# Block-recurrent attention with a mixture-of-depths layer: some turns moved from TensorE to VectorE and through DRAM

## The chip, the cores and the metric

One core of a Trainium2 chip runs the whole kernel. The metric is the device time of one execution in microseconds (us).

## The reference

For 8 batches (B) and 8 heads, x holds 512 rows and the state 32 rows of 64 values. All is float32.

```
scores  = x @ state.T / 8;  a  = softmax(scores);   xread = a @ state     # 512 rows a head
scores2 = state @ x.T / 8;  a2 = softmax(scores2);  sread = a2 @ x        # 32 rows a head
x2[b]   = rows of xread and sread, heads side by side                     # 544 x 512
s       = x2[b] @ w_gate;  top = the 128 rows with the highest s
out[b]  = x2[b];  out[b, top] += sigmoid(s[top]) * (relu(x2[b, top] @ w1) @ w2)   # w1 512x1024, w2 1024x512
```

## The kernel before

Each batch goes through two parts.

*Attention.* x of a batch is loaded as `xf`, 128 partitions by heads, 4 row groups and 64 values. TensorE turns it with the identity, four 128x128 blocks at a time (`turn`, L350), and ScalarE takes each group out of PSUM into `xT` (L359). `scores` (L380) writes scores of both directions into PSUM, state rows on the partitions. For the x rows VectorE turns the scores in 32x32 blocks (L398), takes maximum, difference, sum and product (L402 to L417) and turns them back into `eT` (L420); `read` (L464) makes xread. For the state rows VectorE takes the maximum (L426) and ScalarE the exponential `a` (L430). The second product needs `a` with the x rows on the partitions: TensorE turns it in two groups of four blocks (`turn` in `attention`, L488), ScalarE copies each to `aT` (L491), and `state_read` (L504) makes sread, which ScalarE scales into `xt` (L510). SP stores xread rows (`x_rows`, L531, one DMA) and sread rows (`s_rows`, L536, four DMAs) to the output.

*Choice and layers.* VectorE ranks the rows (`win`, L596; one-hot, L634), TensorE picks the row numbers (L650), POOL gathers the 128 chosen rows back from the output into `xr` (L543). TensorE turns them (L719) into `xg`, the first layer (L736) and the second layer (L753) follow, VectorE adds (`ot`, L756), POOL scatters the rows (L543). The layers are run for batches 0, 1 and 2, 3 and 4, 5 and 6, and 7, two batches side by side as 256 columns.

*The order.* Every step is recorded by `add` with an engine, an assumed length, what it comes after, which buffers it takes and uses, and, for a DMA, how long its data lands after issue (`lands`). `carry_out` then writes all queues out: at each turn it takes the engine that can start first, and on it, among the steps that can start by then, the one with the lowest key, batch number plus an offset by name (`LATER`). The layers have offsets of 100, so that they fill what attention leaves free. A step that waits for a step of another engine counts that step's landing, a step on the same engine does not:

```python
        def since(p, q):
            return end[q] + HOP if q.engine != p.engine else done[q]
```

The queues are in order on the chip. While the first PSUM buffer of the layers is not taken, idle times of TensorE in the plan are filled with small turns of the identity (L160).

Of the kernel before, what the change touches and what calls it, by code (L numbers as in the profile page):

```python
# [8 lines left out]
F32 = mybir.dt.float32  # L9
# [9 lines left out]
def kernel(  # L19
# [10 lines left out]
    nc = tc.nc  # L30
# [4 lines left out]
    SP = S + Ns  # L35
# [19 lines left out]
    def pool(name, bufs, **kw):  # L55
        return ctx.enter_context(tc.tile_pool(name=name, bufs=bufs, **kw))

    N_X, N_XR = 5, 8
    DV = D + 1
    COPIED = ()  # L60
    const = pool("const", 1)
    xin = pool("xin", N_X)
    work = pool("work", 1)
    small = pool("small", 6)
    psum = pool("psum", 1, space=bass.MemoryType.PSUM)


    ctx.enter_context(tc.manual_schedule(engines={ENG.PE, ENG.DVE, ENG.Activation, ENG.SP, ENG.Pool}))
# [3 lines left out]
    SOON = {"PE": 0.0000, "DVE": 0.6720, "ACT": 0.0000, "POOL": 0.0000, "SP": 0.3000, "DMA": 0.0000}  # L72

    LATER = {
        "add": -100.0000, "below": 5.0000, "exp": 5.0000, "exps": -1.1961, "fetch": -2.0379, "first": 100.0000,
        "gate": 0.1040, "gate_s": -0.2629, "heads": -0.5574, "in": -1.6252, "index": -4.8083, "inverse": -1.5775,
        "load": -50.0000, "load_x": -2.0000, "max": 5.0000, "mult": -1.1840, "numbers": 2.7643, "off": -5.0000,
        "oh": -0.9823, "out": -2.8554, "over": -4.8131, "parts": -4.8782, "pick": 3.7775, "picked": -2.5156,
        "plus": -1.1285, "put": -100.0000, "read": 2.4337, "relu": -100.0000, "row": -5.0000, "row_kept": 4.5966,
        "row_s": -4.3556, "row_s_kept": 2.7056, "rows": -4.2797, "score_s": 2.6270, "scores": 1.6993,  # L80
        "second": 100.0000, "sexp": -2.1366, "sigmoid": 4.8122, "smax": -0.6190, "sread": -3.1166, "srows": 2.9423,
        "ssum": -2.6238, "state_T": -4.7221, "state_gates": 2.5691, "states": 1.3988, "store": 3.0032,
        "sub": -4.1349, "sum": -0.5374, "tables": 0.2302, "turn": 0.9682, "turn_a": -2.8074, "turned": -3.8777,
        "turned_a": 3.0201, "twice": 2.0508, "win": -4.7738, "xg": 90.0000, "xg_kept": -100.0000,
    }
    class Buf:

# [12 lines left out]
    class Piece:  # L100
        def __init__(self, engine, length, fn, after, takes, uses, key, lands):
            self.engine, self.length, self.fn, self.lands = engine, length, fn, lands
            self.name, self.key = key[1], key[0] + LATER.get(key[1], 0.0)
            self.after, self.takes, self.uses = [p for p in after if p], takes, uses
            for buf in list(takes) + list(uses):
                buf.users.append(self)
# [58 lines left out]
    def sbuf(name, shape, bufs, dtype=F32, where=None):  # L165
        return Ring(name, shape, dtype, bufs, where)
# [2 lines left out]
    P_SO = Ring("ps_so", [128, 2048], F32, 1, psum)  # L169
    P_H = Ring("ps_h", [128, 512], F32, 2, psum)  # L170
    R_X = Ring("xf", [128, H, NC, D], F32, N_X, xin)
    R_XT = sbuf("xT", [128, 2, 2, 128], 12)
    R_SC = sbuf("s_c", [128, 1024], 1)
    R_E = sbuf("e", [128, 32, Ns], 2)
    R_A = sbuf("a", [128, 2, 2, 256], 1)
    R_ET = sbuf("eT", [128, 2, 2, 2, 128], 2)
    R_AT = sbuf("aT", [128, NC, 128], 2)
    R_XS = sbuf("xs", [128, NC, Dm], 2)
    R_ROW = sbuf("srow", [128, SP], 1)
    R_WIN = [sbuf(f"win{c}", [128, SP - first[c]], 1, BF16) for c in range(NC + 1)]  # L180
# [155 lines left out]
    def attention(b):  # L336

        def key(n):
            return (b, n)
# [3 lines left out]
        for pair in range(H // 2):  # L343
            ps, t = Buf(P_TR), Buf(R_XT)

            def turn(pair=pair, ps=ps):
                v = ps.ap.rearrange("p (k r t) -> p k r t", k=2, r=2)
                for k in range(2):
                    for r in range(2):
                        nc.tensor.transpose(v[:, k, r], xf[b].ap[:, 2 * pair + k, 2 * r:2 * r + 2].rearrange("p w d -> p (w d)"), ident)  # L350

            on = "DVE" if b == 0 and pair % 2 else "ACT"

            def keep(ps=ps, t=t, on=on):
                v = ps.ap.rearrange("p (k r t) -> p k r t", k=2, r=2)
                if on == "DVE":
                    nc.vector.tensor_copy(out=t.ap, in_=v)
                else:
                    nc.scalar.copy(out=t.ap, in_=v)  # L359

            px = p_x[b]
            p = add("PE", 0.66 if b else 0.9, turn, after=[px[(pair * len(px)) // (H // 2)]] + last_turn[-1:], takes=[ps, t], uses=[xf[b]],
                    key=key("turn"))
            last_turn.append(p)
            p_xT.append(add(on, 0.6, keep, after=[p], uses=[ps, t], key=key("turned")))
            xT.append(t)
# [14 lines left out]
                                         xT[2 * g + q // 2].ap[half, q % 2].rearrange("p r t -> p (r t)"),  # L381
                                         start=True, stop=True)

        p_s = add("PE", 1.09, scores, after=p_xT + [p_sT[b]], takes=[s], uses=xT, key=key("scores"))
        if b in COPIED:
            p_s = add("ACT", 1.1, lambda: nc.scalar.copy(out=s_c.ap, in_=s_p.ap[:, 0:1024]), after=[p_s], takes=[s_c], uses=[s],
                      key=key("s_kept"))
# [91 lines left out]
                                uses=[o] + ([xs] if c else []), key=key("rows")))  # L479

        aT, p_aT = [], []
        for g in range(2):
            ps, t = Buf(P_TR), Buf(R_AT)

            def turn(g=g, ps=ps):
                v = ps.ap.rearrange("p (c m) -> p c m", c=NC)
                for c in range(NC):
                    nc.tensor.transpose(v[:, c], a.ap[:, g, c % 2, 128 * (c // 2):128 * (c // 2 + 1)], ident)  # L488
# [23 lines left out]
        p = add("PE", 1.1, state_read, after=p_aT, takes=[o2], uses=aT + [xf[b]], key=key("sread"))  # L512
# [189 lines left out]
    def layers(units, number):  # L702
# [7 lines left out]
        n = at[-1]  # L710
        xg, hT = Buf(R_XG), Buf(R_HT)
        p_xg = []
        for u, lo in zip(units, at):
# [7 lines left out]
            def keep(m=m, pt=pt, lo=lo):  # L721
                nc.scalar.copy(out=xg.ap[:, :, lo:lo + m], in_=pt.ap.rearrange("p (j s) -> p j s", j=ND)[:, :, 0:m])
# [97 lines left out]
```

## Time and profile before

| | |
|---|---|
| median of 3 runs | 217.89 us (217.42 to 218.48) |
| the profiled execution | 215.81 us |
| its span, first to last instruction | 214.0 us |
| granted TensorE clock | 0.999 |
| busy: TensorE, VectorE, ScalarE, POOL | 203.1, 116.3, 89.5, 48.2 us |
| moved by DMA | 26.61 MB, mean 124 GB/s |

The page gives the busy time of each engine, then the span in 40 slices of 5.35 us (a digit is the busy share in tenths), the DMA queues, the chain of work that ended last, the costliest groups and the DMA issues. PE is TensorE's matmul, PEld its weight load, DVE VectorE, ACT ScalarE, SP SyncE; SPq is SP's queue of DMA issues. A float32 matmul of the layers shows as two records, a turn as one.

### The profile page before, as it was taken

Reading aid. Unit: us, or ns where it says so; the run is one execution under the profiler, and the core shown is the slowest. Engines: PE = TensorE matmul, PEld = TensorE weight load, DVE = VectorE, ACT = ScalarE, POOL = GpSimd, SP = SyncE. Lnnn points to the kernel's source line nnn. Section 1 sums busy time; section 2 is a strip of 40 time slices with the busy share of each in tenths; the row PEclk is TensorE's granted clock in tenths of the full one; section 3 lists DMA queues with packets and bytes.
Section 4 is the critical chain, followed back from the end, with each engine's and each line's share of the span. In section 5 each row is a group of like instructions: output and inputs, shape, how many; then the busy total and the mean of one; then the engine's idle time right before and its main releaser. Section 6 shows DMA issues by size and latency. Waiting matters only on the chain.

```text
span 214.0 us, 5364 instructions
## 1 busy us (share of the span) xinstructions
PE 203.1 (95%) x2230; PEld 146.2 (68%) x2230; DVE 116.3 (54%) x271; ACT 89.5 (42%) x196; POOL 48.2 (23%) x139
## 2 busy tenths in 40 slices
PE   6989899999999999999999999999999999999990
PEld 5767676789875568978647667887554887447830
DVE  1499989876686974639987665883340100011001
ACT  2388886973556653534637423534410012000200
POOL 8002010510453021060243115233106200022001
PEclk9999999999999999999999999999999999999999
DMA  7999999629521014043021326102402100011001
GB/s 197 319 307 390 391 360 384 204 77 318 212 54 49 15 49 191 8 142 122 0 61 52 133 83 247 49 9 55 199 0 87 61 3 0 0 49 49 0 0 49
DMA packets 17407, 26.61 MB, mean 124 GB/s; under 512 B 5608, under 2 KB 13800, under 8 KB 16360
## 3 DMA queue, kind: packets, MB, share of 16 engines
q1 hardware_dynamic: 15304, 21.70, 29.4%
q0 software_dynamic: 1280, 4.20, 6.1%
q10 hardware_dynamic: 800, 0.39, 0.7%
q8 instruction: 17, 0.28, 0.6%
q14 instruction: 6, 0.05, 0.1%
HBM read 15.27 MB, written 11.01 MB: 123 GB/s over the span
## 4 chain that ended last, share of the span: by engine, by line
PE 55%; issue 22%; POOL 8%; DVE 6%; ACT 6%; DMA 2%; POOLq 1%; ACTq 0%
PE ps_h L736 14%; PE ps_h L753 13%; PE ps_so L464 7%; PE ps_tr L350 4%; PE ps_tr L504 3%; PE ps_so L380 3%; PE ps_tr L488 3%; POOL xr L543 2%; POOL out_dram L543 2%; ACT a L430 2%; DMA xf<-in_state_dram 2%; PE ps_tr L577 2%; PE ps_tr L623 1%; PE ps_tr L719 1%; ACT xT L359 1%
## 5 line engine op out<-in xcount | busy, mean ns | idle before, releaser
L736 PE MATMUL ps_h<-xg,w 128*128 128x256 f32 (+1 forms) x320 | 60.7, 342 | 0.0
L753 PE MATMUL ps_h<-w,hT 128*128 128x512 f32 x128 | 58.8, 600 | 0.0
L736 PEld LDWEIGHTS ps_h<-xg,w 128*128 128x128 f32 x320 | 50.3, 191 | 6.0 <-issue 1.4
L753 PEld LDWEIGHTS ps_h<-w,hT 128*128 128x128 f32 x128 | 23.0, 190 | 22.9 <-issue 22.5
L756 DVE SCALAR_TENSOR_TENSOR ot<-ps_h,z,xr 128x512 f32<-128x512 f32 x8 | 6.0, 751 | 45.6 <-PE ps_h L753 45.6
L740 ACT ACTIVATE hT<-ps_h 128x512 f32<-128x512 f32 x16 | 9.5, 596 | 44.5 <-PE ps_h L736 44.5
L596 DVE SCALAR_TENSOR_TENSOR win<-srow,sc,after 128x544 bf16<-128x544 f32 (+4 forms) x40 | 18.2, 511 | 15.7 <-ACT srow L586 15.7
L543 POOL DMA_INDIRECT out_dram<-ot,idx x8 | 9.6, 1203 | 63.2 <-DVE ot L756 45.8
L468 ACT COPY xs<-ps_so 128x512 f32<-128x512 f32 x32 | 17.5, 589 | 14.4 <-PE ps_so L464 10.3
L350 PE MATMUL ps_tr<-ident,xf 128*128 128x128 f32 x128 | 20.8, 297 | 0.7 <-ACT xT L359 0.4
L359 ACT COPY xT<-ps_tr 128x512 f32<-128x512 f32 x30 | 17.2, 590 | 7.6 <-PE ps_tr L350 7.0
L464 PE MATMUL ps_so<-st_v,eT 32*128 32x65 f32 x512 | 18.0, 276 | 1.2 <-ACT a L430 0.9
L350 PEld LDWEIGHTS ps_tr<-ident,xf 128*128 128x128 f32 x128 | 14.7, 148 | 6.1 <-ACT xT L359 1.5
L464 PEld LDWEIGHTS ps_so<-st_v,eT 32*128 32x128 f32 x512 | 15.8, 186 | 4.4 <-ACT a L430 1.3
L430 ACT ACTIVATE a<-ps_so,nm 128x512 f32<-128x512 f32 x16 | 10.9, 688 | 7.4 <-DVE nm L426 6.6
L543 POOL DMA_INDIRECT xr<-out_dram,idx x8 | 9.9, 1231 | 16.0 <-DVE sc L566 8.3
L398 DVE STREAM_TRANSPOSE e<-ps_so 128x1024 f32<-128x1024 f32 x8 | 9.9, 1240 | 2.1 <-PE ps_so L380 1.9
L412 DVE TENSOR_REDUCE sm<-e 128x32 f32<-128x1024 f32 x8 | 9.6, 1205 | 2.5 <-ACT e L408 2.5
L420 DVE STREAM_TRANSPOSE eT<-e 128x1024 f32<-128x1024 f32 x8 | 9.9, 1243 | 0.2
L417 DVE TENSOR_TENSOR e<-e,sm 128x1024 f32<-128x1024 f32 x8 | 9.8, 1225 | 0.3
L405 DVE TENSOR_TENSOR e<-e,mx 128x1024 f32<-128x1024 f32 x8 | 9.8, 1223 | 0.2
L488 PE MATMUL ps_tr<-ident,a 128*128 128x128 f32 x64 | 9.5, 280 | 0.3 <-ACT a L430 0.2
(86 smaller groups left out, 220.5 us busy)
## 6 DMA issues: line engine op xcount, KB each, us to landing
out_dram<-xs SPq DMA_DIRECT2D x8, 1024.0 KB, 4.5
xf<-in_x_dram SPq DMA_DIRECT2D x14, 512.0 KB, 7.5
w<-in_moe_w_dram SPq DMA_DIRECT2D x2, 2048.0 KB, 15.7
xf<-in_x_dram SPq DMA_DIRECT2D x3, 256.0 KB, 4.0
out_dram<-xt SPq DMA_DIRECT2D x32, 16.0 KB, 2.8
xf<-in_state_dram SPq DMA_DIRECT2D x1, 384.0 KB, 8.7
xf<-in_x_dram ACTq DMA_DIRECT2D x1, 256.0 KB, 4.6
xf<-in_state_dram ACTq DMA_DIRECT2D x1, 128.0 KB, 3.6
```

What stands on the lines that cost most here:

```text
L350: nc.tensor.transpose(v[:, k, r], xf[b].ap[:, 2 * pair + k, 2 * r:2 * r + 2].rearrange("p w d -> p (w d)"), ident)
L359: nc.scalar.copy(out=t.ap, in_=v)
L398: nc.vector.transpose(out=flat(e), in_=s.ap[:, 0:1024])
L420: nc.vector.transpose(out=eT.ap.rearrange("p w g r t -> p (w g r t)"), in_=flat(e))
L430: nc.scalar.activation(out=a.ap[:, g], in_=view_s()[:, :, g], func=AF.Exp, bias=tmp["nm"][:, g:g + 1], accum_out=tmp["ss"][:, g:g + 1])
L464: nc.tensor.matmul(view(o)[:, q, c - c0, g], eT.ap[r, c % 2, g, c // 2], st_v[r, b, g], start=True, stop=True)
L468: nc.scalar.copy(out=xs.ap[:, c].rearrange("p (g q m) -> p g q m", g=2, q=4), in_=view(o)[:, :, c - c0, :, 0:D].rearrange("p q g m -> p g ...
L488: nc.tensor.transpose(v[:, c], a.ap[:, g, c % 2, 128 * (c // 2):128 * (c // 2 + 1)], ident)
L543: touches(b, nc.gpsimd.indirect_dma_start(**kw), True)
L596: nc.vector.scalar_tensor_tensor(wins[c].ap[0:n], srow.ap[0:n, f:SP], sc[0:n, b, c:c + 1], after[0:n, 0:SP - f], op0=ALU.is_gt, op1=ALU.mu ...
L736: nc.tensor.matmul(v[:, f, 0:n], w1[:, j, 128 * (f0 + f):128 * (f0 + f + 1)], xg.ap[:, j, 0:n], start=(j == 0), stop=(j == ND - 1))
L753: nc.tensor.matmul(py.ap[0:m], hT.ap[:, f, lo:lo + m], w2[:, f], start=(f == 0), stop=(f == NF - 1))
```

## The change

x of batches 6 and 7 is loaded a second time (`load_x2`), in four DMAs a batch of 2048 pieces of 128 bytes, so laid out that VectorE's turn of 32x32 blocks gives `xT` at once. TensorE's turns and ScalarE's copies of these batches are gone; `xf` is still loaded.

`a` of batches 3 to 7 is turned by VectorE in 32x32 blocks into `a_b` (two instructions). The blocks then stand on the wrong partitions: SP stores `a_b` (512 KB) to a DRAM buffer `a_d` and loads it back in four DMAs of 1024 pieces of 128 bytes, each to 32 partitions of `aT2`, which `state_read` uses.

`xg` is laid out with the two batches apart, so that the first layer's moving operand is two runs of 128 columns in place of one of 256. A path that would turn `xr` the same way (`XG_BLOCKS`) is there and empty. Rings of `xT` and `xr` become shorter. Steps of batches 3 and up get names with `_b` and offsets of their own in `LATER`, so the planner writes another order.

```diff
-    N_X, N_XR = 5, 8
+    N_X, N_XR = 5, 6
     DV = D + 1
+    ON_DVE = (6, 7) if cap <= 128 else ()
+    A_BLOCKS = (3, 4, 5, 6, 7) if cap <= 128 else ()
+    XG_BLOCKS = () if cap == 128 else ()
...
+        "a_in_b": 1.5525, "a_out_b": -0.7448, "add": -100.0000, "add_b": -100.0000, "below": 5.0000,
...
-            self.name, self.key = key[1], key[0] + LATER.get(key[1], 0.0)
+            self.name = key[1] + ("_b" if key[0] >= 3 else "")
+            self.key = key[0] + LATER.get(self.name, LATER.get(key[1], 0.0))
...
-    R_XT = sbuf("xT", [128, 2, 2, 128], 12)
+    R_XT = sbuf("xT", [128, 2, 2, 128], 9)
+    R_X2 = sbuf("x2", [128, 2, H, 4, 32], 1)
+    R_AB = sbuf("a_b", [128, 2, NC, 4, 32], 1)
+    R_AT2 = sbuf("aT2", [128, 2, NC, 128], 1)
+    R_AD = Ring("a_d", [128, 2 * NC * 128], F32, 2, dram)
-    R_XG = sbuf("xg", [128, ND, 256], 1)
+    R_XG = sbuf("xg", [128, 2, ND, 128], 1)
...
+    def load_x2(b, key):
+        buf = x2[b] = Buf(R_X2)
+        p_x2[b] = []
+        for w in range(2):
+            for e in range(2):
+                def go(w=w, e=e):
+                    src = x[b].rearrange("h (s t r w) (e d) -> w e t r h s d", s=4, t=32, r=2, e=2)[w, e]
+                    o = 32 * (2 * w + e)
+                    nc.sync.dma_start(out=buf.ap[o:o + 32], in_=src)
+                p_x2[b].append(add("SP", 1.8, go, after=[p_scores[b - 2]], takes=[] if p_x2[b] else [buf],
+                                   uses=[buf] if p_x2[b] else [], key=key, lands=5.0))
...
+            if b in ON_DVE:
+                def turn_blocks(pair=pair, t=t):
+                    nc.vector.transpose(out=t.ap.rearrange("p k r t -> p r k t"),
+                                        in_=x2[b].ap[:, :, 2 * pair:2 * pair + 2].rearrange("p r k s d -> p r k (s d)"))
+                p_xT.append(add("DVE", 0.64, turn_blocks, after=p_x2[b], takes=[t], uses=[x2[b]], key=key("blocks")))
+                xT.append(t)
+                continue
...
+        if b in A_BLOCKS:
+            a_b, a_d, aT2 = Buf(R_AB), Buf(R_AD), Buf(R_AT2)
+            def turn_blocks_a(g):
+                nc.vector.transpose(out=a_b.ap[:, g].rearrange("p (r w) k n -> p w r (k n)", w=2),
+                                    in_=a.ap[:, g].rearrange("p w (r t) -> p w r t", r=2))
+            def a_out():
+                nc.sync.dma_start(out=a_d.ap, in_=a_b.ap.rearrange("p g c k n -> p (g c k n)"))
+            def a_in():
+                for k in range(4):
+                    src = a_d.ap.rearrange("(q t) (z k n) -> k t z q n", q=4, k=4, n=32)[k]
+                    nc.sync.dma_start(out=aT2.ap[32 * k:32 * (k + 1)].rearrange("p g c (q n) -> p (g c) q n", q=4), in_=src)
+            for g in range(2):
+                p_aT.append(add("DVE", 0.66, lambda g=g: turn_blocks_a(g), after=[p_a[g]], takes=[] if g else [a_b],
+                                uses=[a] + ([a_b] if g else []), key=key("blocks_a")))
+            p = add("SP", 0.6, a_out, after=p_aT, takes=[a_d], uses=[a_b], key=key("a_out"), lands=2.2)
+            p_aT = [add("SP", 2.8, a_in, after=[p], takes=[aT2], uses=[a_d], key=key("a_in"), lands=3.0)]
-        for g in range(2):
+        for g in range(0 if b in A_BLOCKS else 2):
...
+                w = lambda j: w1[:, j, 128 * (f0 + f):128 * (f0 + f + 1)]
+                if n == 256:
+                    parts = [(v[:, f].rearrange("p (k s) -> p k s", k=2), xg.ap)]
+                else:
+                    parts = [(v[:, f, at[k]:at[k + 1]], xg.ap[:, k:k + 1, :, 0:u["m"]]) for k, u in enumerate(units)]
...
+        if b in ON_DVE:
+            load_x2(b, (b, "load_x2"))
```

More of the change, by code (lines that the diff above doesn't have):

```diff
@@ L65 @@
     psum = pool("psum", 1, space=bass.MemoryType.PSUM)
+    dram = pool("dram", 1, space=bass.MemoryType.DRAM)
     ctx.enter_context(tc.manual_schedule(engines={ENG.PE, ENG.DVE, ENG.Activation, ENG.SP, ENG.Pool}))
@@ L74 @@
     LATER = {
[L75 to L84, printed above, removed]
+        "a_in_b": 1.5525, "a_out_b": -0.7448, "add": -100.0000, "add_b": -100.0000, "below": 5.0000,
@@ new lines @@
+        "below_b": 4.9516, "blocks_a_b": -3.1491, "blocks_b": 4.2830, "exp": 5.0000, "exp_b": 1.6188,
+        "exps": -1.1961, "exps_b": 1.5285, "fetch": -2.0379, "fetch_b": -4.0717, "first": 100.0000,
+        "first_b": 100.0000, "gate": 0.1040, "gate_b": -0.1483, "gate_s": -0.2629, "gate_s_b": 3.5004,
+        "heads": -0.5574, "heads_b": -4.7153, "in": -1.6252, "in_b": -3.5996, "index": -4.8083, "index_b": -3.6051,
+        "inverse": -1.5775, "inverse_b": 2.5077, "load": -50.0000, "load_x2_b": 1.9782, "load_x_b": -2.2786,
@@ new lines @@
+        "max": 5.0000, "max_b": 4.6396, "mult": -1.1840, "mult_b": 3.4491, "numbers": 2.7643, "off": -5.0000,
+        "off_b": 4.2618, "oh": -0.9823, "oh_b": 4.0841, "out": -2.8554, "out_b": -4.5034, "over": -4.8131,
+        "over_b": 2.4833, "parts": -4.8782, "parts_b": 0.9309, "pick": 3.7775, "pick_b": 4.5229, "picked": -2.5156,
+        "picked_b": 4.7396, "plus": -1.1285, "plus_b": -1.3919, "put": -100.0000, "put_b": -100.0000,
+        "read": 2.4337, "read_b": 4.8884, "relu": -100.0000, "relu_b": -100.0000, "row": -5.0000, "row_b": 2.4330,
@@ new lines @@
+        "row_kept": 4.5966, "row_kept_b": 3.0545, "row_s": -4.3556, "row_s_b": -2.7187, "row_s_kept": 2.7056,
+        "row_s_kept_b": 1.4228, "rows": -4.2797, "rows_b": 4.7760, "score_s": 2.6270, "score_s_b": -4.6623,
+        "scores": 1.6993, "scores_b": 4.0082, "second": 100.0000, "second_b": 100.0000, "sexp": -2.1366,
+        "sexp_b": 1.8469, "sigmoid": 4.8122, "sigmoid_b": 0.5311, "smax": -0.6190, "smax_b": 3.6740,
+        "sread": -3.1166, "sread_b": 3.0414, "srows": 2.9423, "srows_b": 0.4806, "ssum": -2.6238, "ssum_b": -0.7188,
@@ new lines @@
+        "state_T": -4.7221, "state_T_b": -3.3351, "state_gates": 2.5691, "state_gates_b": 4.7733, "states": 1.3988,
+        "states_b": 4.5170, "store": 3.0032, "store_b": 1.3222, "sub": -4.1349, "sub_b": -4.5526, "sum": -0.5374,
+        "sum_b": -2.8598, "tables": 0.2302, "turn": 0.9682, "turn_a": -2.8074, "turn_b": 3.1911, "turned": -3.8777,
+        "turned_a": 3.0201, "turned_b": 3.5876, "twice": 2.0508, "win": -4.7738, "win_b": -5.0000, "xg": 90.0000,
+        "xg_b": 90.0000, "xg_kept": -100.0000, "xg_kept_b": -100.0000,
@@ L177 @@
     R_AT = sbuf("aT", [128, NC, 128], 2)
+    R_AB = sbuf("a_b", [128, 2, NC, 4, 32], 1)
+    R_AT2 = sbuf("aT2", [128, 2, NC, 128], 1)
+    R_XB = sbuf("x_b", [128, ND, 4, 32], 1)
+    R_AD = Ring("a_d", [128, 2 * NC * 128], F32, 2, dram)
+    R_XD = Ring("x_d", [128, Dm], F32, 2, dram)
     R_XS = sbuf("xs", [128, NC, Dm], 2)
@@ L266 @@
     make_identity(nc, ident)
-    xf, p_x, last_load = {}, {}, []
+    xf, p_x, last_load, x2, p_x2, p_scores = {}, {}, [], {}, {}, {}
     def load_x(b, key, pieces=2):
@@ L382, in scores @@
                                          start=True, stop=True)
-        p_s = add("PE", 1.09, scores, after=p_xT + [p_sT[b]], takes=[s], uses=xT, key=key("scores"))
+        p_s = p_scores[b] = add("PE", 1.09, scores, after=p_xT + [p_sT[b]], takes=[s], uses=xT, key=key("scores"))
         if b in COPIED:
@@ L503, in state_read @@
                         rr = slice(Ns * q, Ns * (q + 1))
-                        nc.tensor.matmul(o2.ap[rr, D * g:D * (g + 1)], aT[g].ap[:, c, rr], xf[b].ap[:, 4 * g + q, c],
+                        nc.tensor.matmul(o2.ap[rr, D * g:D * (g + 1)], (aT[g].ap if aT else aT2.ap[:, g])[:, c, rr], xf[b].ap[:, 4 * g + q, c],
                                          start=(c == 0), stop=(c == NC - 1))
@@ L510, in state_rows @@
                 nc.scalar.activation(out=tmp["xt"][:, g], in_=o2.ap[:, D * g:D * (g + 1)], func=AF.Copy, scale=tmp["rs"][:, g:g + 1])
-        p = add("PE", 1.1, state_read, after=p_aT, takes=[o2], uses=aT + [xf[b]], key=key("sread"))
+        p = add("PE", 1.1, state_read, after=p_aT, takes=[o2], uses=(aT or [aT2]) + [xf[b]], key=key("sread"))
         p_xt = add("ACT", 0.42, state_rows, after=[p, p_rs], uses=[o2], key=key("srows"))
@@ L712, in layers @@
         p_xg = []
-        for u, lo in zip(units, at):
+        for k, u in enumerate(units):
             m, pt = u["m"], Buf(P_TR)
@@ L719, in turn, with keep, turn_blocks_x, x_out @@
                     nc.tensor.transpose(v[:, j, 0:m], u["xr"].ap[0:m, 128 * j:128 * (j + 1)], ident[0:m, 0:m])
-            def keep(m=m, pt=pt, lo=lo):
-                nc.scalar.copy(out=xg.ap[:, :, lo:lo + m], in_=pt.ap.rearrange("p (j s) -> p j s", j=ND)[:, :, 0:m])
+            def keep(m=m, pt=pt, k=k):
+                nc.scalar.copy(out=xg.ap[:, k, :, 0:m], in_=pt.ap.rearrange("p (j s) -> p j s", j=ND)[:, :, 0:m])
+            if u["b"] in XG_BLOCKS:
+                x_b, x_d = Buf(R_XB), Buf(R_XD)
+                def turn_blocks_x(u=u, x_b=x_b):
+                    nc.vector.transpose(out=x_b.ap.rearrange("p j e s -> p (j e s)"), in_=u["xr"].ap)
+                def x_out(x_b=x_b, x_d=x_d):
+                    nc.sync.dma_start(out=x_d.ap, in_=x_b.ap.rearrange("p j e s -> p (j e s)"))
+                def x_in(x_d=x_d, k=k):
+                    for e in range(4):
+                        src = x_d.ap.rearrange("(q d) (j e s) -> e d j q s", q=4, e=4, s=32)[e]
+                        nc.sync.dma_start(out=xg.ap[32 * e:32 * (e + 1), k].rearrange("p j (q s) -> p j q s", q=4), in_=src)
+                key_b = (u["b"], "blocks_x"), (u["b"], "x_out"), (u["b"], "x_in")
+                p = add("DVE", 0.66, turn_blocks_x, after=[u["got"]], takes=[x_b], uses=[u["xr"]], key=key_b[0])
+                p = add("SP", 0.6, x_out, after=[p], takes=[x_d], uses=[x_b], key=key_b[1], lands=2.2)
+                p_xg.append(add("SP", 2.4, x_in, after=[p], takes=[] if p_xg else [xg], uses=[x_d] + ([xg] if p_xg else []),
+                                key=key_b[2], lands=2.5))
+                continue
             p = add("PE", 0.52, turn, after=[u["got"]], takes=[pt], uses=[u["xr"]], key=key("xg"))
@@ L734, in first_layer @@
                 v = ph.ap.rearrange("p (f s) -> p f s", f=nf)
-                for j in range(ND):
-                    nc.tensor.matmul(v[:, f, 0:n], w1[:, j, 128 * (f0 + f):128 * (f0 + f + 1)], xg.ap[:, j, 0:n],
-                                     start=(j == 0), stop=(j == ND - 1))
+                w = lambda j: w1[:, j, 128 * (f0 + f):128 * (f0 + f + 1)]
[3 more added lines that the diff above has]
+                    parts = [(v[:, f, at[k]:at[k + 1]], xg.ap[:, k:k + 1, :, 0:u["m"]]) for k, u in enumerate(units)]
+                for o, i in parts:
+                    for j in range(ND):
+                        nc.tensor.matmul(o, w(j), i[:, :, j] if n == 256 else i[:, 0, j], start=(j == 0), stop=(j == ND - 1))
             def relu(f0=f0, ph=ph):
```

## The prediction

> **What bounds the kernel now.** I read the page's busy shares first, then the chain of waits in order of time, then the timelines of VectorE and of SP's queue, then the DMA issues.
>
> ```profile
> PE 203.1 (95%) x2230; PEld 146.2 (68%) x2230; DVE 116.3 (54%) x271; ACT 89.5 (42%) x196; POOL 48.2 (23%) x139
> PE   6989899999999999999999999999999999999990
> DVE  1499989876686974639987665883340100011001
> ```
>
> TensorE is busy from the third slice to the last; its longest single wait in the list of waits is 1.3 us, at the start. VectorE fills only the slices up to 55 us (in 15 to 35 us it is busy 18.3 of 20), so there TensorE fills its time with early turns and warm-up transposes. After 70 us the chain is TensorE alone, and the turns of `a` stand in it:
>
> ```profile
> 76.79 0.44 PE ps_tr L488 x4
> 86.43 0.59 PE ps_tr L488 x4
> 101.87 0.44 PE ps_tr L488 x4
> 103.33 0.59 PE ps_tr L488 x4
> 112.79 0.87 PE ps_tr L488 x8
> 137.82 1.01 PE ps_tr L488 x8
> ```
>
> Columns: start, length, what. A group of four costs 0.44 us behind another of its kind and 0.59 behind 32-row work. The chain has no stage after 70 us where TensorE waits long, so what is taken from TensorE there comes off the end, unless it turns into a wait.
>
> **What is taken from TensorE.** The `a` turns of batches 3 to 7 are ten groups. Eight are the rows above: 0.44+0.59+0.44+0.59+0.87+1.01 = 3.9 us. Batch 3's two groups (at 63.2 and 65.4) took 1.0. The x turns of batches 6 and 7 are the last eight groups of L350, between 56.4 and 72.4 us: 4.3 us by their distances to the next instruction. Together 9.2 us. In the new order three x groups of batch 5 (1.3 us) slip from the early stage into this one, 1.8 us of first-layer work goes the other way, and twelve warm-ups stand where eleven were: about 0.2 us worse than even, since the stage from 38 to 55 is itself nearly full. I take 9.0 us. ScalarE loses 18 evictions of 0.59 us; it is 42% busy, so that is worth nothing by itself.
>
> **What VectorE gets.** A block turn of 512 columns is half of this row's 1240 ns:
>
> ```profile
> L398 DVE STREAM_TRANSPOSE e<-ps_so 128x1024 f32<-128x1024 f32 x8 | 9.9, 1240 | 2.1 <-PE ps_so L380 1.9
> ```
>
> 18 of 0.62 us are 11.2 us more. From 70 to 150 us VectorE is 70% busy (page of windows: 14.6, 15.7, 12.9 and 13.3 of 20), so this lies in its gaps. Where it is late: three of batch 6's x turns stand ahead of batch 3's win, 1.9 us, but the row that win needs comes late in any case (VectorE's idle time before win at 86 us was 3.19). Without that cover it would cost 1.9 us.
>
> **The first layer's operand** is now two runs of 128 columns in place of 256. Nothing of before shows that form. Its 192 records follow at 0.216 us (12.09 us for 56); 128-column records at 0.112 (7.14 us for 64). Between 0 and 192 x 0.008 = 1.5 us; a gain is excluded, as the columns are the same. I take 0, since one instruction reads them.
>
> **The trip through DRAM.** This is what decides. The state read of batches 3 to 7 waits no longer for a ScalarE copy but for VectorE's turn, a 512 KB store, and four loads of 1024 pieces of 128 bytes. Rows that bound it:
>
> ```profile
> out_dram<-xs SPq DMA_DIRECT2D x8, 1024.0 KB, 4.5
> ```
>
> ```profile
> q1 hardware_dynamic: 320, 0.07, 9.9%
> issues: line engine op xcount, KB each, median us to landing
> out_dram<-xt SPq DMA_DIRECT2D x4, 16.0 KB, 1.8
> ```
>
> The second fence is the DMA view for 142 to 146 us, where one batch's small stores are alone: 320 packets take 9.9% of 16 x 4 us, 20 ns each, and land 1.8 us after issue. The store of `a_b` lies halfway between 1.8 and 4.5: 3.1. The four loads go out one by one, 0.58 us apart (the median issue on L536), and 1024 packets at 20 ns on 16 engines are 1.3 us: 3 x 0.58 + 1.8 + 1.3 = 4.9. The trip is 8.0 us. From below: 1.8 for the store and 1.8 + 1.3 with all four loads issued at once: 4.9. From above: 4.5, and the loads data-bound at 0.6 + 4 x 1.3 + 1.4 = 7.2: 11.7.
>
> [...]
>
> **How long TensorE has before it needs each trip.** The planner counts no landing between two steps of one queue, so it put the state read 6.4 us after the block turn. Now the walk, with TensorE's pieces by their rows (layer piece 1.73, or 1.92 behind 32-row work; read 1.05; scores 1.02; state read 1.03).
>
> ```profile
> 62.15 1.21 DVE L402 TENSOR_REDUCE mx<-e 128x32 f32<-128x1024 f32 x1
> 63.39 1.22 DVE L405 TENSOR_TENSOR e<-e,mx 128x1024 f32<-128x1024 f32 x1
> 69.72 3.35 SPq L536 DMA_DIRECT2D out_dram<-xt  x4
> 90.90 2.92 SPq L536 DMA_DIRECT2D out_dram<-xt  x4
> 142.21 2.49 SPq L536 DMA_DIRECT2D out_dram<-xt  x4
> ```
>
> - Batch 3: VectorE goes from the subtraction (64.6) into the block turns, done at 66.0. TensorE: scores of batch 4 from 64.2, when batch 3's exps free PSUM, to 65.3; two second-layer pieces, 3.6; a turn of `xr` and its copy, 1.2; three first-layer pieces, 1.92 + 1.73 + 1.73: state read at 75.5. Room 9.5 less a hop, 9.4.
> - Batch 4: SP stores batch 3's state rows ahead of this trip. State read of 3 at 75.5, ScalarE first does two exps for batch 4 (to 76.9), state rows to 77.4, four stores at 2.9 us by the three rows, to 80.3. TensorE: it may read again when batch 4's exps free PSUM, 76.9; then read 1.05, layers 3.65, sums 0.2, read 0.95, layer 1.92, row 0.6, read 0.95 and hops: 86.4. Room 6.1: the store is stuck behind other stores, not behind VectorE (78.6).
> - Batch 5: VectorE has batch 1's `ot` ahead of the block turns, and that waits for a second layer's end, S. 0.75 + 1.3 + hops: store at S + 2.3. TensorE: scores 1.1, `xr` turn 0.44, second layer 3.63, turn 0.44, second layer 3.63: S + 9.3. Room 7.0.
> - Batch 6: again behind the state rows of the batch before. From batch 5's state read R: store at R + 4.5 (1.03, ScalarE 0.55, SP 2.9); TensorE 1.03 + 1.92 + 0.95 + 0.2 + 1.92 + 0.95 + 1.92 + 0.6 + 1.73 = 11.2, with a hop R + 11.3. Room 6.8.
> - Batch 7: scores end T; store at T + 9.3 (in, offsets, one-hot, three passes of 1.2, exps, turn), TensorE 2.9 to the rank sums, then 1.9 + 0.3 + 5.3 + 1.73 + 0.44 + 3.6 + 1.05: T + 17.2. Room 7.9.
>
> At 8.0 us the waits are 0 + 1.9 + 1.0 + 1.2 + 0.1 = 4.2 us, and each further microsecond costs four. Queued behind: everything on TensorE, whose queue is in order; on SP also the big row stores of the batch, which wait behind the four loads, but whose gather comes some 10 us later. The 16,384 small packets of x for batches 6 and 7 are 10 us of DMA time each by the same 20 ns; they are issued at 55, at 73 to 77 and at 92 to 103 us, where the DMA share of before is about 0.2 or less for all but the first, and their turns come some 7 us later or more.
>
> Sum: -9.0 + 4.2 = -4.8 us. Against the profiled execution: 215.8 (span 214.0 and 1.8 around) becomes 211.0. It lies 2.1 below the median of the runs, 217.9; taken off the median the forecast is 213.1.
>
> **Rivals.**
> - The trip is covered: at 6 us or less no state read waits, 217.9 - 9.0 = 208.9. For it: DMA is nearly idle after 70 us. Against: the chain has two DMA latencies in a row.
> - Slower: the trip is longer than I take it. From 9.2 us on the waits (4 x 9.2 - 27.8 = 9.0) eat the whole gain. At 10.5 they are 1.1 + 4.4 + 3.5 + 3.7 + 2.6 = 15.3, and the time is 224.2. [...] Against: 20 ns is already a 256-byte packet.
> - The x turns are worth nothing, since from 55 to 70 us the chain runs over POOL's gathers and VectorE. Then only 5.0 comes off: 217.1. Against: TensorE is busy 9.3 of 10 us there.
> - Two runs of 128 cost 1.5 us: a shift of the others, in the range.
>
> **How the numbers follow.** Forecast 0.37 (own range 210.5 to 216.5), covered 0.27, long trip 0.21, x turns worthless 0.09, the rest 0.06 on both sides. The range goes from the covered case less 1.4 for shorter waits elsewhere, 207.5, into the long trip at about 9.9 us, 221.0. A measurement of this kernel tells about 0.5%, 1.1 us, from no change. Faster: the forecast nearly whole, covered, a little of the others: 0.66. Same 0.09: x turns worthless, the forecast's upper edge. Slower 0.25: long trip and mishaps.
>
> **What would show it.** Right: TensorE's busy time lower by about 9 us, the state read of batches 4, 5 and 6 idle before it for 1 to 2 us each on a DMA of `aT2`, trip near 8 us, VectorE near 127 us. Wrong: state reads that do not wait (covered), or that wait over 3 us each; first-layer records over 384 ns; TensorE idle on VectorE between 70 and 150 us.

## The result: 225.6 us, 3.7% slower, and the profile after

The changed kernel took 225.63 us (median of 4 runs, 224.95 to 228.04), the kernel before 217.88 beside it: ratio 1.037, 95% interval 1.029 to 1.045. Ratios here are of runs within 1.5% of the fastest of their kernel; medians are of all runs. The profiled execution took 224.95 us, its span 223.2; before it was 215.81 and 214.0. So 9.2 us of span are to be explained, where the prediction had 4.8 us less. The time lies above the range given, which ended at 221.0.

The page of the kernel after, busy shares, slices of TensorE and VectorE, and the granted clock:

```profile
PE 200.3 (90%) x2159; PEld 141.7 (64%) x2159; DVE 126.4 (57%) x289; ACT 81.3 (36%) x178; POOL 49.8 (22%) x139
PE   6899898699998998299996999999969999999990
DVE  2589999744687999235999189649911430011001
PEclk9999999969999999589999699999996999999999
```

Before, TensorE's row had no digit under 8 between its first and its last. Now there are holes at slices 8, 17, 22 and 30, and in the row of the clock a fall within or just after each of them. The list of waits of TensorE names what it waited for (total us, times, longest):

```profile
PE ps_tr L569 <- DMA aT<-a_d: 9.7, 3, 5.0
PE ps_tr L784 <- DMA xr<-out_dram,idx: 1.6, 1, 1.6
```

L569 is the state read, L784 the turn of the gathered rows. TensorE's timeline, state reads of batches 4, 5 and 7 (start, length, what, idle time before it and its releaser):

```profile
93.45 1.94 PE L569 MATMUL ps_tr<-xf,aT 128*32 128x64 f32 x64 [5.00 <-DMA aT<-a_d]
122.94 1.10 PE L569 MATMUL ps_tr<-xf,aT 128*32 128x64 f32 x64 [2.15 <-DMA aT<-a_d]
167.88 1.41 PE L569 MATMUL ps_tr<-xf,aT 128*32 128x64 f32 x64 [2.51 <-DMA aT<-a_d]
```

Those of batches 3 and 6 did not wait. The same read takes 1.10 in one row and 1.94 in another; the windows around the longest wait (busy times of TensorE, its weight loads, VectorE, ScalarE, POOL, then the clock, DMA share and GB/s) show why:

```profile
88.00:90.00 2.00, 0.45 (x17) 0.31 (x12) 2.00 (x8) 1.20 (x4) 0.00 (x0) 1.00 0.51 81
92.00:94.00 2.00, 0.55 (x23) 0.58 (x26) 0.00 (x0) 0.00 (x0) 0.00 (x0) 0.50 1.06 387
94.00:96.00 2.00, 2.00 (x55) 1.74 (x47) 0.00 (x1) 0.52 (x2) 0.00 (x0) 0.50 0.39 164
98.00:100.00 2.00, 2.00 (x51) 1.86 (x51) 1.18 (x4) 0.07 (x1) 0.00 (x0) 1.00 0.15 35
```

After the wait, TensorE works on at half the clock (0.50) for some 2 to 4 us. The prediction had no such term. By the rows that ran slow, against the same pieces at full clock, it cost: state read and first-layer piece of batch 4, 0.85 + 0.75; the first-layer piece behind the wait of batch 5, 3.65 for 1.99, 1.65; state read and second-layer piece of batch 7, 0.3 + 1.35; and 24 first-layer records at 45.89 us, 4.44 for 2.94, 1.5, behind the 1.6 us wait for gathered rows. Together 6.4 us. One of these pieces, and below it the same at full clock:

```profile
123.97 3.65 PE L828 MATMUL ps_h<-xg,w 128*128 128x256 f32 x8
128.75 1.99 PE L828 MATMUL ps_h<-xg,w 128*128 128x256 f32 x8
```

The account of the span: -8.1 of turns (see below), -0.7 of a start that was quicker in this execution (the state read at 31.35 us before stands at 30.64), +9.7 waits for the trip, +1.6 wait for the gathered rows, +6.4 low clock: +8.9, measured +9.2.

How long the trip was, from SP's queue (start, issue time, what). It shows batch 3's trip, then what stood ahead of batch 4's, then that trip, whose loads landed at 93.36:

```profile
68.86 0.33 SPq L534 DMA_DIRECT2D a_d<-a_b  x1
71.49 2.85 SPq L539 DMA_DIRECT2D aT<-a_d  x4
74.39 5.10 SPq L317 DMA_DIRECT2D x<-in_x_dram  x3
79.68 4.64 SPq L601 DMA_DIRECT2D out_dram<-xt  x4
84.42 0.53 SPq L534 DMA_DIRECT2D a_d<-a_b  x1
87.30 3.10 SPq L539 DMA_DIRECT2D aT<-a_d  x4
```

From issue of the store to landing of the last load: 8.9 us for batch 4, 8.9 for batch 5 (113.90 to 122.81), 10.05 for batch 7 (157.70 to 167.75). The packets themselves fill only part of that. The DMA view for 117.2 to 122.9 us, where batch 5's four loads are alone, has

```profile
q1 hardware_dynamic: 4160, 0.52, 60.4%
```

or 13 ns a packet, 3.4 us on 16 engines, of the 5.6 us that the loads took.

### The profile page after: what moved, and what is told of

It is laid out like the page before. It is cut to its first block, busy times and chain, and to the rows that moved or that the text cites. A ratio compares the mean times of both kernels' runs of the same rounds, so it can differ in the third digit from the quotient of the medians.

```text
span 223.2 us, 5270 instructions
## 1 busy us (share of the span) xinstructions
PE 200.3 (90%) x2159; PEld 141.7 (64%) x2159; DVE 126.4 (57%) x289; ACT 81.3 (36%) x178; POOL 49.8 (22%) x139
## 4 chain that ended last, share of the span: by engine, by line
PE 54%; issue 16%; DMA 10%; DVE 10%; ACT 4%; SPq 3%; POOL 2%; POOLq 1%
PE ps_h L828 21%; PE ps_h L844 10%; PE ps_so L508 6%; DMA aT<-a_d 5%; PE ps_so L424 4%; PE ps_tr L569 3%; SPq L539 3%; PE ps_tr L386 2%; DMA xr<-out_dram,idx 2%; DMA a_d<-a_b 2%; DVE e L442 2%; PE ps_tr L642 2%; DMA xf<-in_state_dram 1%; PE ps_tr L688 1%; DVE nm L470 1%
## 5 line engine op out<-in xcount | busy, mean ns | idle before, releaser
L828 PE MATMUL ps_h<-xg,w 128*128 128x256 f32 (+1 forms) x320 | 65.3, 359 | 0.7 <-ACT xg L787 0.7
L828 PEld LDWEIGHTS ps_h<-xg,w 128*128 128x128 f32 x320 | 52.8, 202 | 7.6 <-issue 1.1
L661 DVE SCALAR_TENSOR_TENSOR win<-srow,sc,after 128x544 bf16<-128x544 f32 (+4 forms) x40 | 18.2, 512 | 10.5 <-ACT srow L651 10.4
L608 POOL DMA_INDIRECT out_dram<-ot,idx x8 | 10.5, 1309 | 52.5 <-DVE ot L847 33.9
L569 PE MATMUL ps_tr<-xf,aT 128*32 128x64 f32 x512 | 9.9, 236 | 9.7 <-DMA aT<-a_d 9.7
L608 POOL DMA_INDIRECT xr<-out_dram,idx x8 | 11.4, 1430 | 25.7 <-DVE idx L719 22.5
L569 PEld LDWEIGHTS ps_tr<-xf,aT 128*32 128x32 f32 x512 | 8.6, 120 | 11.8 <-issue 8.4
L386 PE MATMUL ps_tr<-ident,xf 128*128 128x128 f32 x96 | 14.8, 284 | 1.1 <-ACT xT L403 0.4
L403 ACT COPY xT<-ps_tr 128x512 f32<-128x512 f32 x22 | 12.7, 590 | 5.9 <-PE ps_tr L386 5.5
L672 POOL CAST aux<-sc 128x5 bf16<-128x5 f32 x8 | 1.6, 200 | 57.7 <-DVE sc L516 57.7
L386 PEld LDWEIGHTS ps_tr<-ident,xf 128*128 128x128 f32 x96 | 10.2, 140 | 4.4 <-ACT xT L403 1.1
```

What stands on the lines that cost most here:

```text
L569: nc.tensor.matmul(o2.ap[rr, D * g:D * (g + 1)], (aT[g].ap if aT else aT2.ap[:, g])[:, c, rr], xf[b].ap[:, 4 * g + q, c], start=(c == 0), ...
L608: touches(b, nc.gpsimd.indirect_dma_start(**kw), True)
L661: nc.vector.scalar_tensor_tensor(wins[c].ap[0:n], srow.ap[0:n, f:SP], sc[0:n, b, c:c + 1], after[0:n, 0:SP - f], op0=ALU.is_gt, op1=ALU.mu ...
L828: nc.tensor.matmul(o, w(j), i[:, :, j] if n == 256 else i[:, 0, j], start=(j == 0), stop=(j == ND - 1))
```

## Experiments

Four questions: is it the wait for the trip; is the low clock an effect of the waits; which part of the change is to blame; what makes the trip long. Each group of runs had its own runs of the kernel before beside it (medians 216.1 to 217.0), so kernels are best compared by their ratios.

**No wait for the trip.** All DMAs and block turns stay, and so does the order of every engine; the state reads of batches 3 to 7 take columns of `w1` as weights, so that sread of these batches is left out.

```diff
-    (aT[g].ap if aT else aT2.ap[:, g])[:, c, rr]
+    (aT[g].ap[:, c, rr] if aT else w1[:, c, 128 * g + Ns * q:128 * g + Ns * (q + 1)])
```

> The state reads of batches 3 to 7 take columns of w1 as weights and not the turned ones, so they wait for nothing that the trip brings; order, block turns, stores and loads of the trip all stay. Theory 1 (the loss is TensorE waiting for the trip, and the low clock after each such wait): its waits of 9.7 us at L569 go, and the 5.2 us that TensorE lost at the low clock after them: 225.6 - 14.9 = 210.7 us. If the low clock has nothing to do with the waits, only 9.7 go: 215.9. Rival (the many small transfers slow everything beside them, whoever waits): over 220.

Measured 211.47 us, ratio 0.970 (0.965 to 0.976). The whole loss is the waiting and what follows it. What the traffic by itself costs is small at most: TensorE's only waits for a DMA are then two for gathered rows, of 1.66 and 0.64 us, and the first of them ends before any x block is loaded. The fall of 14.2 us is more than the 9.7 of waits: the clock came back with them, from 0.962 to 0.985, and what is left of the fall while TensorE works stands behind the 1.66 us.

**TensorE kept busy while it waits.**

```diff
         def state_read():
+            for _ in range({4: 44, 5: 18, 7: 21}.get(b, 0)):
+                nc.tensor.transpose(o2.ap[:, 256:384], ident, ident)
...
+                for _ in range(14 if u["b"] == 0 else 0):
+                    nc.tensor.transpose(pt.ap[:, 0:128], ident, ident)
```

> TensorE is given turns of the identity that nobody reads, in the places where it waits: 44, 18 and 21 ahead of the state reads of batches 4, 5 and 7, and 14 ahead of the turn of batch 0's gathered rows. The waits stay as long as they are. Theory 2 (an idle TensorE is granted half the clock for some microseconds afterwards, and that is 6.7 of the 9.2 us lost in the span): the clock stays near 1.0 and the time falls to 225.6 - 6.7 = 218.9. Rival (the clock falls for another reason, or turns do not keep it up): no change, 225. [...]

Measured 221.95 us, ratio 1.022 (1.017 to 1.026), 3.7 us less than the changed kernel (3.4 by the ratios), though TensorE does 97 turns more. The clock was 0.993 to 0.999 in its four runs, where the changed kernel's four had 0.962 to 0.975. The windows, for the same place as above:

```profile
90.00:92.00 2.00, 2.00 (x21) 2.00 (x20) 0.24 (x3) 0.00 (x0) 0.00 (x0) 1.00 0.69 108
94.00:96.00 2.00, 2.00 (x29) 1.56 (x18) 0.92 (x3) 0.52 (x2) 0.00 (x0) 1.00 0.31 123
```

From 88.10 to 93.18 TensorE did nothing but turns, and the clock stayed at 1.00. Where TensorE sat idle in this place, in the changed kernel, it was 0.50 from 90 to 96 us. So here the idle time lowered it, and turns kept it up. Only some 3.5 of the 6.4 us came back, since the trips of batches 5 and 6 came late in this run and left a wait of 1.30 us behind the fillers of batch 5 and one of 1.33 at batch 6, which had none; the clock did not fall behind these (the first-layer pieces that follow took 1.99 us both times, as at full clock).

**Each part alone**, with 12 buffers of `xT` as before.

```diff
-    ON_DVE = (6, 7) if cap <= 128 else ()
+    ON_DVE = ()
-    N_X, N_XR = 5, 6
+    N_X, N_XR = 5, 8
-    R_XT = sbuf("xT", [128, 2, 2, 128], 9)
+    R_XT = sbuf("xT", [128, 2, 2, 128], 12)
```

> Only the weights' part: x of batches 6 and 7 is turned by TensorE again, xT has 12 buffers and xr 8 as before the change, so that the early stage is in the order of before. Theory 1 (the trip itself is too long): five groups of two turns less on TensorE, -4.9 us by the prediction's rows, the waits of batches 5 and 7 stay (4.7 us), that of batch 4 falls by about 3 as no x2 loads stand ahead of its store on SP (2.0), and each is followed by some 1 us of low clock: 217.9 - 4.9 + 6.7 + 3.0 = 222.7. Rival (the x2 loads on SP and the missing xT buffers are what made the waits): 213 to 215.

The weights' part alone: 224.2 us, ratio 1.030 (1.024 to 1.036). Theory 1 holds. In its profile, of the longest of the four runs (227.6 us), all five state reads wait, 9.6 us in all, the longest 3.64, for trips of 8.8 to 9.8 us, though no load of x blocks stands on SP.

```diff
-    A_BLOCKS = (3, 4, 5, 6, 7) if cap <= 128 else ()
+    A_BLOCKS = ()
-    R_XT = sbuf("xT", [128, 2, 2, 128], 9)
+    R_XT = sbuf("xT", [128, 2, 2, 128], 12)
```

> Only the x part: the turns of a go back to TensorE and ScalarE, x of batches 6 and 7 is turned by VectorE, xT has 12 buffers. Theory 1 (x turns leave TensorE without a new wait): -4.3 us by the prediction's rows, 213.6 us. Rival (they are worth nothing, since the chain of 55 to 70 us goes over POOL and VectorE): 217.9. Rival 2 (the 16,384 small packets and the block turns on VectorE make a new wait): over 219.

The x part alone: 213.23 us, ratio 0.983 (0.980 to 0.986), 3.8 us faster than before; 4.3 were expected. The rivals fall. So the change is a good half and a bad one.

**The x part with 9 buffers**: as the last, without the line of `R_XT`.

> Only the x part, as in the run with 12 buffers of xT (213.2 us), but with the 9 buffers that the change leaves. Theory 3 (with 9 buffers, the turns of batch 5 that kept TensorE busy while batch 0's rows were fetched can't be placed there, and this costs 3.0 us, as the scores of batch 3 start 3.0 us later in the changed kernel): 216.2. Rival (what is late there is caught up later): 213.2.

Measured 213.22 us, ratio 0.986 (0.981 to 0.991): the same as with 12. Theory 3 falls in the form it was given. The scores of batch 3 do start 1.2 us later than with 12 buffers (56.43 against 55.21), but not 3.0, and the end does not show it. The turn of the gathered rows in this run, and below it in the run without waits for the trip:

```profile
44.13 0.63 PE L784 MATMUL ps_tr<-ident,xr 128*128 128x128 f32 x4 [0.59 <-DMA xr<-out_dram,idx]
```

```profile
45.07 0.63 PE L784 MATMUL ps_tr<-ident,xr 128*128 128x128 f32 x4 [1.66 <-DMA xr<-out_dram,idx]
```

With 0.59 us of idle time the clock did not fall (1.00 from 42 to 52 us); with 1.66 it did (0.61 and 0.53 in the two windows of 46 to 50 us), as with 1.60 in the changed kernel. The gather's issue took POOL 1.22 us here and 2.1 there. That 9 buffers leave this gather uncovered is shown; why its length differs is open.

**Fewer, longer pieces.** First the four loads as plain rows; the blocks then stay where VectorE left them, so that sread of batches 3 to 7 is not what it should be:

```diff
-    src = a_d.ap.rearrange("(q t) (z k n) -> k t z q n", q=4, k=4, n=32)[k]
-    nc.sync.dma_start(out=aT2.ap[32 * k:32 * (k + 1)].rearrange("p g c (q n) -> p (g c) q n", q=4), in_=src)
+    rows = slice(32 * k, 32 * (k + 1))
+    nc.sync.dma_start(out=aT2.ap[rows].rearrange("p g c n -> p (g c n)"), in_=a_d.ap[rows])
```

> The changed kernel, whose four loads of the trip fetch the same bytes as 32 rows of 4 KB each and not as 1024 pieces of 128 bytes; the blocks so stay where VectorE left them, and the state rows of batches 3 to 7 are left out of the reading of the output. Theory P (the number of pieces makes the trip long): the loads land 1.8 to 2.2 us after their issue and not 3.7 to 3.9, the trip of 8.9 to 10 us loses 1.7, the three waits lose 5.1 of their 9.7 and some 2.5 of the low clock with them: about 218. Rival (two landings in a row and four issues one after the other make it, whatever the pieces): landing over 3 us, 224 to 226.

Measured 215.88 us, ratio 0.994 (0.990 to 0.998). The DMA issues of the page, first of the changed kernel, then of this run (KB each, median us to landing):

```profile
a_d<-a_b SPq DMA_DIRECT2D x5, 512.0 KB, 2.6
aT<-a_d SPq DMA_DIRECT2D x20, 128.0 KB, 3.9
```

```profile
a_d<-a_b SPq DMA_DIRECT2D x5, 512.0 KB, 3.6
aT<-a_d SPq DMA_DIRECT2D x20, 128.0 KB, 2.8
```

The loads land in 2.8 us and follow each other at 0.36 to 0.47 us, not 0.64 to 1.06. The trip of batch 4 is 7.5 us, of batch 5 7.8, of batch 7 8.3. The pieces are worth 1.1 to 1.8 us a trip: the waits at the state read are 6.0 us in place of 9.7, the clock falls behind one of them (2.52 us, with 3.78 us for the first-layer piece that follows) and not behind three (1.98 or 1.99 for the piece of a layer that follows), and the time falls by nearly 10 us. Even so two landings in a row leave 7.5 us.

Then the same in a form that computes everything: `a_b` with the block column outermost, so that a partition's share of one load is four runs of 1 KB (the state read picks its weights from that layout, not shown).

```diff
-    R_AB = sbuf("a_b", [128, 2, NC, 4, 32], 1)
-    R_AT2 = sbuf("aT2", [128, 2, NC, 128], 1)
+    R_AB = sbuf("a_b", [128, 4, 2, NC, 32], 1)
+    R_AT2 = sbuf("aT2", [128, 4, 2, NC, 32], 1)
...
-    nc.vector.transpose(out=a_b.ap[:, g].rearrange("p (r w) k n -> p w r (k n)", w=2),
-                        in_=a.ap[:, g].rearrange("p w (r t) -> p w r t", r=2))
+    nc.vector.transpose(out=a_b.ap[:, :, g].rearrange("p k c n -> p c k n"),
+                        in_=a.ap[:, g].rearrange("p w (r k n) -> p (w r) k n", r=2, k=4))
...
+    src = a_d.ap.rearrange("(q t) (k m) -> k t q m", q=4, k=4)[k]
+    nc.sync.dma_start(out=aT2.ap[32 * k:32 * (k + 1)].rearrange("p q g c n -> p q (g c n)"), in_=src)
```

> The changed kernel with a_b, its DRAM copy and aT2 laid out so that what one load fetches for a partition is four runs of 1 KB and not 32 of 128 bytes; the state read picks its weights from that layout, so the whole is computed. Theory P (the number of pieces lengthens the trip, as the run with 4 KB rows showed: load issues 0.4 apart and landing in 2.8, trip 7.6 to 9.0 us): nearly the same with 512 pieces a load set as with 128, 216. Rival (it is the straight rows of that run, partition by partition, and not the piece length): over 220.

Median 217.4 us over ten runs, 213.1 to 220.4 but for one of 382.2, with 216.1 before: the spread is too wide to tell it from the kernel before. The profiled run took 216.25. Its loads land in 3.0 and follow at 0.36 to 0.49 us, and the waits at the state read are 6.1 us. So 1 KB is nearly as good as 4 KB for issue and landing. The spread goes with the clock: 213.06 us at 0.996, 220.43 at 0.970. In the profiled run the clock did not fall behind the longest of these waits, TensorE's for batch 4:

```profile
91.68 1.10 PE L569 MATMUL ps_tr<-xf,aT 128*32 128x64 f32 x64 [3.09 <-DMA aT<-a_d]
90.00:92.00 2.00, 0.32 (x23) 0.35 (x26) 0.66 (x7) 0.00 (x0) 0.00 (x0) 1.00 0.97 399
92.00:94.00 2.00, 2.00 (x63) 1.78 (x52) 0.61 (x3) 0.52 (x2) 0.00 (x0) 1.00 0.15 61
```

So a wait can bring the low clock (0.50 at that of 5.00 us in the changed kernel) and need not (1.00 behind this one of 3.09).

**The loads of the x blocks on another queue.**

```diff
-    nc.sync.dma_start(out=buf.ap[o:o + 32], in_=src)
+    nc.scalar.dma_start(out=buf.ap[o:o + 32], in_=src)
```

> The changed kernel, but the blocks of x of batches 6 and 7 are loaded from ScalarE's queue and not from SP's; all else is in the same order. Theory 4 (three of these loads hold SP for 5.1 us ahead of batch 4's trip): batch 4's wait of 5.0 us falls by about 3, and 0.9 of low clock with it: 221.5. Rival (the issues only move, and hold ScalarE's state rows or evictions for as long): 225 or more.

Measured 228.26 us, ratio 1.056 (1.051 to 1.061): slower than the changed kernel. TensorE's timeline, batches 3 and 4, and one window (last but one column: DMA share as busy time of 2.00):

```profile
81.97 1.71 PE L569 MATMUL ps_tr<-xf,aT 128*32 128x64 f32 x64 [4.63 <-DMA aT<-a_d]
95.83 1.10 PE L569 MATMUL ps_tr<-xf,aT 128*32 128x64 f32 x64 [0.18 <-issue]
```

```profile
74.00:76.00 2.00, 2.00 (x11) 1.77 (x10) 1.97 (x3) 0.28 (x1) 1.59 (x3) 1.00 1.61 140
```

Batch 4's wait goes from 5.0 to 0.2, but not as theory 4 has it. In the changed kernel the x loads were off SP at 79.49 us, and the state rows that come next on SP were ready only then, by ScalarE's row:

```profile
79.13 0.52 ACT L575 ACTIVATE xt<-ps_tr,rs 128x64 f32<-128x64 f32 x2 [0.16 <-PE ps_tr L569]
```

What changed is that the four stores of state rows now take 2.50 us and not 4.64, so that batch 4's store follows the state read of batch 3 by 4.9 us and not 6.5. The other 3.4 us of room came from TensorE, which did the pieces between the two reads slower: 1.99 us for a read that takes 1.12 at full clock, and 5.47 for 16 first-layer records that take 3.72. For batch 3, which did not wait, now waits 4.63. Both sets of 128-byte pieces are under way together, the DMA engines are 80% busy at 140 GB/s, and the last load of batch 3 lands 7.84 us after its issue, where 3.9 was the median. SP's queue had put one behind the other.

**An order planned with longer trips.**

```diff
-    p = add("SP", 0.6, a_out, ..., lands=2.2)
-    p_aT = [add("SP", 2.8, a_in, ..., lands=3.0)]
+    p = add("SP", 0.4, a_out, ..., lands=3.0)
+    p_aT = [add("SP", 6.0, a_in, ..., lands=3.7)]
-                add("SP", 0.4, s_rows, ..., lands=2.5)]
+                add("SP", 2.9, s_rows, ..., lands=2.5)]
```

> The changed kernel with three lengths of the planner set to what the trace shows: the store of a_b 0.4 us on SP and landing in 3.0, the loads 6.0 on SP (waiting for the store included) and landing in 3.7, the four stores of state rows 2.9 and not 0.4. Theory 1 (the order left the trips too little room, since it was planned with too short a trip): the state reads no longer wait, 225.6 - 14.9 = 210.7, and up to 4 us more for what the new order loses elsewhere: 211 to 215. Rival (TensorE has no work that could fill a trip of 9 to 10 us, so that the wait only moves, to the last batches above all): over 219.

Measured 222.05 us, ratio 1.029 (1.023 to 1.034): the rival. No state read waits any more. But TensorE has a new wait, longer than any before; the turn of the last gathered rows:

```profile
162.51 1.09 PE L784 MATMUL ps_tr<-ident,xr 128*128 128x128 f32 x4 [6.85 <-DMA xr<-out_dram,idx]
```

That the layers' pieces that now cover the trips are what is missing here is argued, not shown.

**Trips only where none had waited.**

```diff
-    N_X, N_XR = 5, 6
+    N_X, N_XR = 5, 4
-    A_BLOCKS = (3, 4, 5, 6, 7) if cap <= 128 else ()
+    A_BLOCKS = (3, 6) if cap <= 128 else ()
-    R_XT = sbuf("xT", [128, 2, 2, 128], 9)
+    R_XT = sbuf("xT", [128, 2, 2, 128], 12)
```

> The x part with 12 buffers of xT (213.2 us), and the weights' trip only for batches 3 and 6, whose state reads never waited for it in the changed kernel; 4 buffers of xr, so that all fits. Theory 1 (a trip with 10 us of room costs nothing): four turn groups less, 213.2 - 2.0 = 211.2. Rival (each trip costs even there, by the order that it forces): 213 to 217.

Measured 215.53 us, ratio 0.995 (0.993 to 0.997), some 2 us above the x part alone: the rival. That batches 3 and 6 had room in one order does not give it to them in another; batch 6's state read now waits 2.27 us, batch 3's 0.51.

**Shorter trips with room planned for them**: 1 KB pieces, 12 buffers of `xT`, 4 of `xr`, and

```diff
+    p = add("SP", 0.4, a_out, ..., lands=3.0)
+    p_aT = [add("SP", 4.4, a_in, ..., lands=2.8)]
```

> As the run with 1 KB pieces, and the order made with 12 buffers of xT, 4 of xr, and lengths of the trip nearer to the trace: store 0.4 us and landing in 3.0, loads 4.4 (waiting for the store included) and landing in 2.8. Theory 1 (a trip that is shorter than the room it is given costs nothing): the time of the run whose state reads do not wait, 211.5, less the early stage's 1.6 us wait and its low clock: 209 to 212. Rival (other stores and x loads on SP take the room away again): 214 to 218.

Measured 212.47 us, ratio 0.984 (0.977 to 0.992), against 1.037 for the changed kernel. One wait for the trip is left, batch 4's, whose store stands on SP right behind the state rows of batch 3 (77.31 to 81.15 us):

```profile
89.81 1.93 PE L569 MATMUL ps_tr<-xf,aT 128*32 128x64 f32 x64 [3.76 <-DMA aT<-a_d]
```

**The same without batch 4's trip.**

```diff
-    A_BLOCKS = (3, 4, 5, 6, 7) if cap <= 128 else ()
+    A_BLOCKS = (3, 5, 6, 7) if cap <= 128 else ()
```

> As the run with 1 KB pieces and more room (212.5 us), with batch 4 left to TensorE and ScalarE: its state read was the only one that still waited there, 3.8 us, with some 2 us of low clock behind it. Theory 1 (what is lost is that one wait, and a trip with room costs nothing): 212.5 - 3.8 - 2.0 + 1.0 for batch 4's own turns = 207.7. Rival (the wait goes to another batch, or x loads and state rows on SP take the room of batch 3 or 5 in the new order): 211 to 214.

Measured 210.34 us, ratio 0.970 (0.966 to 0.974): faster than both kernels. No state read waits. The page:

```profile
PE 196.2 (94%) x2166; PEld 139.9 (67%) x2166; DVE 125.8 (60%) x287; ACT 81.9 (39%) x180; POOL 49.3 (24%) x139
PEclk9999999999999999999999999999999999999999
```

Its span is 208.4, 5.6 us under that of before, and the clock never falls in this execution. The 207.7 expected was 2.6 too low.

## Why the prediction was wrong, point by point

- **Turns off TensorE, -9.0.** Nearly right, and real: the run without waits has 196.5 us of busy TensorE for 203.1, 6.6 less, and 1.5 of low clock stands in it: 8.1. Where the other 0.9 went is open. The rival that x turns are worth nothing fell, 3.8 us of 4.3.
- **The trip, 8.0 us.** Mis-sized. The store was taken at 3.1 and was 2.9, 3.3 and 3.7. The loads were taken at 4.9 and were 6.1, 5.6 and 6.3: a load of 128-byte pieces was issued every 0.64 to 1.06 us, not 0.58, and the last one landed in 3.5 to 4.1 us, where 1.8 + 1.3 was taken. The row of 20 ns a packet came from small stores that were alone (64 of the 320 packets were of 4 bytes; those of 256 bytes took 22 ns) and held nothing of what 1024 pieces add to issue and landing; the packets themselves were quicker than that, 13 ns.
- **The rooms.** Near in sum. A trip less its wait gives 3.9 for batch 4 (6.1 predicted), 6.7 for batch 5 (7.0) and 7.5 for batch 7 (7.9); batch 6 had 9.0 where 6.8 was given, 1.7 of it by the first-layer piece that ran slow behind batch 5's wait. For batch 4 the step that failed is what stands on SP: the state-row stores took 4.64 us and not 2.9, which is 1.7 of the 2.2 that were missing. The three loads of x blocks ahead of them, priced as DMA time only, held SP for 5.10 us but were done when the state rows were. With no x loads ahead on SP, in the weights' part alone and in the run with the other queue, these stores took 2.50; that x blocks still under way slow them is argued from that, not shown.
- **The price of a wait.** This is the step that failed most. A wait of TensorE was counted at its own length. Put the measured trips of 8.9, 8.9 and 10.05 us against the predicted rooms, with 8.9 for batch 6: 2.8 + 1.9 + 2.1 + 2.2 = 9.0 us of waits, and the sum would still have been near nothing, 0.0. The low clock behind the waits, 6.4 us, and the early wait of 1.6, of which the prediction says only that the stage was nearly full, make up most of the rest. How much low clock comes is in part chance: the same kernel's runs differ in it (granted clock 0.962 to 0.975 in the four of the changed kernel), and a wait of 3.09 us in the run with 1 KB pieces brought none.
- **The rivals.** The long trip had the right mechanism and 224.2 us, but reached that by waits of 15.3 us at a trip of 10.5; measured were 9.7 us at 8.9 to 10.05, and the clock made up the difference. Its break-even, a trip of 9.2, was too high: with the low clock, trips of 7.0 to 8.9 us (4 KB pieces) came out at 0.994 of before.
- **Right:** VectorE 126.4 us for 127; the two-run operand costs nothing (16 records in a row take 3.72 us before and after; the mean of 403 ns, over the 384 given as a sign of being wrong, came with the low clock, and the run without waits for the trip has 388); TensorE's waits lie on `aT2` and not on VectorE. The forecast for the state read of batch 6, a wait, did not hold.

## What to carry to other kernels

Before a step is moved off a busy TensorE onto a path with two DMA landings, count the time between producer and consumer in the order that will be written, with every issue that stands on the same queue, and reckon that a miss can cost more than its length: here 11.3 us of waits brought 6.4 us of half clock with them, though not every wait in the other runs did. The change's good part could be had by itself, and its other part became a gain too once the trip was shorter (1 KB pieces), given room by the planner, and left out where there was none: 3.0% under the kernel before, where all of it together was 3.7% above.

## What the runs showed of the hardware

- In the changed kernel all four long waits of TensorE, of 1.60, 2.15, 2.51 and 5.00 us, were followed by about half the granted clock (0.50 to 0.54 in two-microsecond windows), within the wait of 5.00 us itself, from 90 us on, and 1 to 2 us after the end of those of 1.60 and 2.15, for 2 to 4 us. In the weights' part alone TensorE ran slow for some 10 us behind a wait of 2.35 (a second-layer piece took 3.78 us and a later one 3.42, for 1.98 at full clock). But length alone does not settle it: the clock stayed at 1.00 behind a wait of 3.09 (1 KB pieces), and the first-layer piece behind waits of 2.50 (x loads on the other queue) and 1.67 us (4 KB pieces) took 1.99 us, as at full clock. Behind the state reads' waits of 1.30, 1.33, 1.44 and 1.50 us (with turns as fillers, and in the weights' part alone) the next piece of a layer took 1.98 or 1.99 us too. So 1.60 was enough in one place, and 3.09 was not in another. What decides is open.
- Turns of a 128x128 identity, 0.114 us apart, kept the clock at 1.00 through 5 us in which TensorE did nothing else.
- Loads of 128 KB in 1024 pieces of 128 bytes were issued every 0.64 to 1.06 us in the changed kernel, and the last of four landed in 3.5 to 4.1; in 128 pieces of 1 KB every 0.36 to 0.49 and in 3.1 to 3.8; in 32 of 4 KB in 2.7 to 3.3. Beside another stream of 128-byte pieces the first kind landed in 7.84 us.
